# Another order for the middle of a planned RWKV-7 and mixer kernel, and transposes as pairs of 64-row blocks

## The chip, the core and the metric

The kernel runs on one core of a Trainium2 chip. The metric is device time in microseconds of one launch, read and written in HBM. Times are the median of several executions; a profile is one further execution, recorded by the hardware profiler.

The core has five engines with a queue each. PE (TensorE) does matrix products and transposes and writes to PSUM, a memory of eight banks. DVE (VectorE) and ACT (ScalarE) read PSUM and write to SBUF. POOL (GpSimd) works on SBUF alone. SP (SyncE) issues most DMAs. Each engine takes its queue in order and waits for others by semaphores.

## What is computed

Two stages. The first is a recurrence over 768 steps for 4 batches of 8 heads with a state of 40 by 40 per head:

```python
for t in range(S):
    y[:, :, t] = np.einsum('bhd,bhde->bhe', rt, state)
    Sa = np.einsum('bhde,bhe->bhd', state, at)
    state_decay = state * wt[:, :, None, :] - np.einsum('bhd,bhe->bhde', Sa, bt)
    state = state_decay + np.einsum('bhd,bhe->bhde', vt, kt)
```

The second takes the heads side by side (x, 768 by 320 for each batch) through a mixer:

```python
theta = x @ w_theta
zr, zi = x * np.cos(theta), x * np.sin(theta)
y = np.einsum('ts,bsd->btd', w_tok_r, zr) + np.einsum('ts,bsd->btd', w_tok_i, zi)
u = x + y
return u + np.maximum(u @ w_ch, 0.0)
```

## The kernel before

**Tiling.** The 768 steps of a batch are six chunks of 128, so there are 24 chunks, numbered 0 to 23 through all batches. Inside a chunk the recurrence is written as products of triangular score matrices; from chunk to chunk a state (`gt`, and its turned copy `gd`) is handed on. For chunk i the operations are, with the names that the text uses (kind and chunk, `tkb8`):

- loads `lw lk lb la lv` and `loadr` (SP);
- `ln`, `cs`, `exp`, `cx` or `wi`, `ew`: sums of the logarithms of w and their exponentials;
- `kb` (two), `ah`, `v`, `r`: products or casts into padded bf16 tiles with 64 columns for each head, mostly on POOL;
- transposes on PE: `tkb` (eight blocks of 128x128 from k and b), `ta` and `tv` (four each), `tr` (eight, for two chunks at once), `nut` (four), and for the mixer `xt` and `ut` (five each for two chunks); `wt` (six) turns rows of the token weights. Each is copied from PSUM to SBUF by ACT or DVE: `ekb ea ev er enut ext eut ewt`;
- scores on PE: `spsi sphi slv slu`, eight matmuls of 64 rows and 128 columns each. The two halves of the rows hold two heads, and write two different PSUM banks. `mpsi mphi mlv mlu` multiply them by a triangular mask on DVE, or copy them on ACT, after which `sel` cuts the triangle on POOL;
- the recurrence: `x0`, `nx`, `nu`, `enu`, `gt`, `egt`, `wgt`, `gd`, `egd`; the readout `y` and `ex`;
- the mixer: `th` and `eth` (theta), `sin` (sine and cosine on ACT, with a change of activation table), `z` (x times cosine or sine, on POOL or DVE, two for each chunk), `row` (the products over tokens, six steps for each chunk), `uadd`, `ch`, `oo`, `st`.

`thj` and `chj` are the last part of a product that is shared by two chunks, on 64 rows.

**The order.** The code adds 1602 operations to a plan with what each reads and writes (`Plan.add`, L161), then emits them in the order of a list of numbers, `ORDER` (L26). Only the order within an engine's queue has an effect; waits between engines follow from the data. `HOMES` (L122) gives each new PSUM tile its bank, in order of emission. `PICK` (L138) names the operations that run on their second choice of engine. `WARM` (L145) puts some matmuls on a constant ahead of early operations. All of these lists are written out in the file.

**PSUM.** Banks 0 to 3 are two tiles of two banks each (`doubles`), which the scores use; banks 4 to 7 are four single tiles. A transpose takes one bank. `scores` (L558) writes `ps(p)[:, q]`, bank q for half q of the rows. A transpose in the code before goes through `transpose_pairs` or a loop of its own:

```python
nc.tensor.transpose(out=dst[:, c:c + 128], in_=pair(src, g), identity=ident)
```

ACT copies its result as 32-bit words, DVE as 16-bit elements (`copy_words` and `copy_halves`, both used by `evac`).

Of the kernel before, what the change touches and what calls it, by code (L numbers as in the profile page):

```python
# [26 lines left out]
    0, 7, 3, 6, 1, 2, 20, 8, 21, 23, 24, 4, 27, 9, 32, 30, 5, 22, 31, 33, 12, 25, 26, 34, 11,  # L27
    28, 10, 69, 35, 36, 29, 70, 37, 18, 47, 44, 40, 19, 48, 72, 45, 38, 41, 71, 49, 73, 39, 46,
    98, 119, 76, 99, 58, 14, 42, 100, 74, 57, 15, 13, 120, 122, 101, 50, 121, 79, 75, 51, 123,
    53, 106, 102, 107, 131, 108, 80, 52, 16, 77, 109, 132, 125, 78, 43, 103, 81, 17, 110, 134,  # L30
    126, 111, 133, 82, 56, 84, 137, 54, 104, 124, 138, 112, 129, 83, 85, 87, 130, 88, 127, 55,
    156, 86, 128, 59, 157, 89, 146, 184, 143, 90, 147, 105, 158, 61, 97, 60, 139, 187, 159,
    135, 62, 144, 148, 164, 96, 188, 160, 165, 191, 140, 93, 136, 145, 161, 166, 141, 91, 185,
    167, 213, 186, 92, 194, 214, 149, 189, 142, 162, 168, 150, 215, 163, 169, 190, 216, 195,
    152, 221, 170, 234, 151, 246, 192, 222, 235, 193, 237, 217, 95, 236, 202, 238, 218, 94,
    196, 203, 197, 63, 241, 155, 247, 171, 267, 248, 219, 239, 199, 198, 172, 220, 223, 205,
    249, 200, 240, 271, 64, 244, 272, 242, 299, 245, 201, 154, 273, 224, 243, 300, 173, 301,
    261, 206, 254, 274, 302, 225, 174, 262, 303, 279, 153, 175, 258, 306, 176, 255, 212, 259,
    263, 280, 250, 177, 204, 281, 256, 211, 275, 496, 282, 260, 320, 226, 251, 305, 257, 208,
    252, 276, 264, 283, 253, 317, 207, 227, 349, 327, 265, 277, 497, 328, 304, 309, 278, 329,  # L40
    498, 284, 266, 310, 270, 499, 330, 350, 285, 307, 351, 268, 318, 286, 354, 308, 269, 331,
    352, 500, 311, 361, 332, 319, 287, 314, 353, 312, 209, 336, 333, 539, 362, 210, 337, 289,
    356, 288, 315, 363, 313, 322, 290, 364, 338, 355, 291, 387, 325, 292, 339, 316, 365, 540,
    388, 359, 366, 389, 541, 357, 360, 340, 390, 341, 382, 358, 391, 321, 116, 503, 113, 501,
    542, 412, 373, 181, 342, 334, 376, 374, 502, 392, 367, 411, 326, 504, 377, 375, 506, 335,
    393, 368, 505, 323, 178, 369, 545, 524, 394, 378, 370, 507, 517, 525, 413, 508, 372, 526,
    384, 371, 509, 395, 416, 396, 527, 532, 417, 528, 397, 510, 511, 514, 529, 544, 117, 595,
    512, 572, 533, 415, 383, 530, 118, 398, 573, 515, 596, 513, 554, 385, 399, 534, 531, 574,
    418, 597, 401, 535, 400, 516, 575, 414, 402, 543, 379, 324, 404, 114, 567, 598, 536, 403,
    546, 548, 115, 380, 581, 642, 576, 582, 555, 601, 549, 577, 381, 583, 599, 66, 386, 550,  # L50
    584, 537, 557, 568, 600, 551, 182, 522, 558, 602, 183, 585, 586, 538, 619, 578, 561, 587,
    419, 179, 518, 559, 547, 604, 519, 556, 427, 180, 428, 421, 429, 605, 560, 420, 606, 520,
    423, 552, 607, 626, 553, 562, 434, 422, 627, 564, 435, 425, 436, 565, 563, 643, 628, 424,
    437, 644, 610, 566, 629, 426, 613, 645, 603, 588, 611, 630, 231, 523, 571, 521, 589, 438,
    430, 570, 698, 635, 631, 646, 612, 439, 431, 636, 632, 440, 608, 745, 432, 614, 699, 647,
    609, 746, 700, 675, 648, 747, 637, 433, 615, 676, 616, 701, 293, 569, 633, 677, 748, 634,
    651, 649, 638, 678, 590, 652, 684, 296, 579, 685, 679, 617, 639, 228, 620, 621, 580, 653,
    706, 657, 591, 654, 680, 592, 618, 686, 650, 593, 661, 703, 687, 594, 441, 622, 711, 702,
    640, 442, 681, 712, 662, 688, 655, 658, 705, 656, 689, 659, 641, 663, 660, 682, 704, 664,
    690, 749, 667, 683, 665, 691, 68, 709, 692, 707, 67, 710, 729, 668, 65, 670, 672, 666, 708,  # L60
    694, 693, 750, 624, 695, 730, 719, 713, 697, 751, 720, 731, 696, 232, 732, 294, 233, 297,
    714, 721, 295, 733, 738, 298, 229, 734, 739, 715, 716, 230, 740, 735, 717, 754, 450, 752,
    451, 778, 755, 718, 346, 625, 452, 779, 453, 741, 343, 623, 756, 881, 780, 454, 757, 408,
    882, 781, 742, 405, 673, 671, 764, 883, 767, 765, 669, 782, 884, 444, 722, 455, 783, 443,
    768, 456, 766, 445, 784, 446, 736, 457, 885, 785, 458, 760, 737, 743, 447, 459, 753, 448,
    786, 787, 887, 744, 761, 796, 788, 769, 758, 460, 759, 789, 763, 461, 888, 762, 790, 462,
    797, 912, 463, 792, 791, 913, 793, 723, 770, 795, 892, 771, 914, 794, 674, 893, 915, 886,
    772, 802, 890, 464, 891, 803, 773, 347, 465, 916, 348, 344, 799, 917, 905, 805, 409, 345,
# [133 lines left out]
def mm(n):  # L202
    return max(n / 2.4 + 2.5, 25.0)
# [853 lines left out]
```

## Time and profile before

| | us |
|---|---|
| runs | 197.72, 198.29, 202.19 |
| median | 198.29 |
| span of the profiled execution | 197.8 |

The profile comes from an execution of its own, whose whole time is not listed; its span, from the first to the last instruction, lies between the lowest and the middle one of the three runs. On the profile's page, engines are named as above, with PEld for the weight loads that run beside the matmuls. An engine's busy time is the union of its instructions; for PE the end of each matmul is modelled. A line such as L391 may be that of a helper and stand for several kinds of operations. In the groups, a row gives line, engine, operation, what is written from what, shapes, count, total time, the mean of one in ns, and the idle time ahead of them with what ended it. In a timeline, a row gives start, length of the group, engine, line and count.

### The profile page before, as it was taken

The page shows a single profiled execution, that of the slowest core. Times are in us where ns is not written, and L with a number is a line of the kernel's source. Part 1 is how long each engine was busy: PE and PEld are TensorE (multiplying, and loading weights), DVE is VectorE, ACT ScalarE, POOL GpSimd, SP SyncE. Part 2 cuts the span into 40 slices and gives each one's busy share as a digit, 9 for nine tenths or more (in the row PEclk, how much of TensorE's full clock was granted, in tenths as well). Part 3 has the DMA queues.
Part 4 walks back from the last instruction along what each step waited for, and adds up shares of the span by engine and source line. Part 5 has one row for each costly group of instructions (what it writes and reads, how often), then busy time and mean ns, then how long its engine had stood idle before and what let it go on. Part 6 is the DMA issues. An engine that isn't in the chain of part 4 may idle for free.

```text
span 197.8 us, 8019 instructions
## 1 busy us (share of the span) xinstructions
PE 187.6 (95%) x3288; PEld 150.3 (76%) x3288; DVE 164.3 (83%) x261; ACT 151.7 (77%) x337; POOL 145.1 (73%) x210
## 2 busy tenths in 40 slices
PE   7888999999989999999999999999999999999992
PEld 6776787777768788878878888888887878767661
DVE  5269899999989999888887988999999988675453
ACT  3584979799889988979988598888998986575111
POOL 8267544679879999699799939769699697558100
PEclk9999999999999999999999999999999999999999
DMA  6999879989999999999998899988998274863055
GB/s 119 210 212 163 154 161 196 182 166 197 233 174 173 207 171 185 190 185 223 153 210 168 153 187 170 188 148 169 182 155 163 43 177 102 87 194 104 0 191 174
DMA packets 134644, 32.75 MB, mean 166 GB/s; under 512 B 124816, under 2 KB 134608, under 8 KB 134608
## 3 DMA queue, kind: packets, MB, share of 16 engines
q1 hardware_dynamic: 131680, 29.19, 75.1%
q0 software_dynamic: 2784, 2.97, 9.6%
q8 instruction: 25, 0.41, 0.9%
q10 hardware_dynamic: 144, 0.08, 0.1%
q14 instruction: 11, 0.09, 0.1%
HBM read 29.54 MB, written 3.93 MB: 169 GB/s over the span
## 4 chain that ended last, share of the span: by engine, by line
PE 68%; DMA 9%; ACT 8%; SPq 6%; DVE 3%; issue 3%; POOL 1%; ACTq 0%; DVEq 0%; POOLq 0%
PE ps_s L881 17%; PE ps_s L391 10%; PE ps_d L569 9%; PE ps_s L763 5%; SPq L409 4%; DMA raw_w<-in_w_dram 3%; DMA raw_kb<-in_k_dram 3%; PE ps_s L711 3%; PE ps_s L652 2%; PE ps_s L629 2%; SPq L421 2%; DMA raw_r<-in_r_dram 2%; PE ps_s L538 2%; PE ps_s L773 2%; ACT cs L850 2%
## 5 line engine op out<-in xcount | busy, mean ns | idle before, releaser
L429 POOL TENSOR_TENSOR kb<-raw_kb,ex 128x320 bf16<-128x320 f32 x46 | 36.8, 811 | 9.7 <-DMA raw_kb<-in_k_dram 3.3
L881 PE MATMUL ps_s<-zr,wtok_r 128*128 128x320 bf16 x132 | 37.6, 299 | 0.0
L881 PE MATMUL ps_s<-zi,wtok_i 128*128 128x320 bf16 x132 | 37.5, 299 | 0.0
L578 DVE TENSOR_TENSOR lamu<-ps_d,mask_p 128x1024 bf16<-128x1024 f32 x22 | 26.8, 1219 | 1.7 <-PE ps_d L569 1.6
L578 DVE TENSOR_TENSOR psi<-ps_d,mask_p 128x1024 bf16<-128x1024 f32 x22 | 26.8, 1218 | 1.6 <-PE ps_d L569 1.4
L578 DVE TENSOR_TENSOR lamv<-ps_d,mask_p 128x1024 bf16<-128x1024 f32 x17 | 20.7, 1218 | 2.6 <-PE ps_d L569 1.8
L429 POOL TENSOR_TENSOR ah<-raw_a,we 128x320 bf16<-128x320 f32 x22 | 19.0, 866 | 3.6 <-DMA raw_a<-in_a_dram 1.6
L578 DVE TENSOR_TENSOR phi<-ps_d,mask_n 128x1024 bf16<-128x1024 f32 x17 | 20.7, 1218 | 0.9 <-PE ps_d L569 0.8
L865 POOL TENSOR_TENSOR zi<-cs,xp 128x320 bf16<-128x320 f32 x21 | 16.9, 816 | 3.3 <-ACT cs L850 3.3
L881 PEld LDWEIGHTS <-wtok_r 128*128 128x128 bf16 x144 | 14.0, 97 | 4.5
L569 PE MATMUL ps_d<-aT,kbT 64*128 64x128 bf16 x384 | 17.1, 217 | 0.2
L881 PEld LDWEIGHTS <-wtok_i 128*128 128x128 bf16 x144 | 14.1, 98 | 3.5
L391 PE MATMUL ps_s<-wide,kb 128*128 128x128 bf16 x184 | 15.0, 223 | 1.0 <-POOL kb L429 0.7
L865 POOL TENSOR_TENSOR zr<-cs,xp 128x320 bf16<-128x320 f32 x19 | 15.3, 810 | 0.7 <-ACT cs L850 0.7
L667 POOL TENSOR_TENSOR gt<-sum,ex 128x320 bf16<-128x320 f32 x13 | 9.5, 733 | 8.0 <-DVE sum L663 4.8
L800 PE MATMUL ps_s<-kb,lamv 128*128 128x40 bf16 x192 | 15.0, 180 | 0.0
L802 PE MATMUL ps_s<-kb,lamu 128*128 128x40 bf16 x192 | 14.9, 179 | 0.0
L569 PEld LDWEIGHTS <-kbT 64*128 64x128 bf16 x384 | 11.8, 94 | 3.1 <-ACT kbT L394 1.0
L800 PEld LDWEIGHTS <-lamv 128*128 128x128 bf16 x192 | 13.2, 96 | 0.6
L887 DVE TENSOR_TENSOR up<-ps_s,xp 128x320 bf16<-128x320 f32 x22 | 10.7, 488 | 3.5 <-PE ps_s L881 3.1
L435 POOL CAST r<-raw_r 128x640 bf16<-128x640 f32 x12 | 8.6, 720 | 6.5 <-DMA raw_r<-in_r_dram 6.5
L445 ACT ACTIVATE lw<-raw_w 128x320 bf16<-128x320 f32 x24 | 11.4, 475 | 2.6 <-DMA raw_w<-in_w_dram 2.6
(176 smaller groups left out, 606.7 us busy)
## 6 DMA issues: line engine op xcount, KB each, us to landing
raw_w<-in_w_dram SPq DMA_DIRECT2D x24, 160.0 KB, 4.1
raw_v<-in_v_dram SPq DMA_DIRECT2D x24, 160.0 KB, 3.9
raw_a<-in_a_dram SPq DMA_DIRECT2D x24, 160.0 KB, 4.2
raw_kb<-in_k_dram SPq DMA_DIRECT2D x24, 160.0 KB, 3.7
raw_kb<-in_b_dram SPq DMA_DIRECT2D x24, 160.0 KB, 4.0
raw_r<-in_r_dram SPq DMA_DIRECT2D x24, 160.0 KB, 4.4
out_dram<-oo SPq DMA_DIRECT2D x9, 160.0 KB, 2.0
wrow_i<-in_moe_w_tok_i_dram POOLq DMA_DIRECT2D x6, 192.0 KB, 5.3
```

The costliest lines, as they stand in the source:

```text
L391: nc.tensor.transpose(out=dst[:, c:c + 128], in_=pair(src, g), identity=ident)
L429: pool = ("POOL", lambda: nc.gpsimd.tensor_tensor(out=dst, in0=in0, in1=in1, op=ALU.mult))
L445: add("ACT", "ln", i, lambda: nc.scalar.activation(out=paired(lw)[:, :, :, 0:D], in_=paired(raw_w[s4]), func=AF.Ln), 473, [("raw_w", s4)], ...
L569: nc.tensor.matmul(t[:, q, g, :], lhsT=lhs[g][rows(q)], rhs=rhs[g][rows(q)], start=True, stop=True)
L578: add("DVE", kindm, i, lambda: nc.vector.tensor_tensor(out=flat, in0=whole(), in1=mask.to_broadcast([128, 2 * G, 128]), op=ALU.mult), 1217 ...
L667: add("POOL", "wgt", i, lambda: nc.gpsimd.tensor_tensor(out=new_state, in0=sum_t, in1=wm.to_broadcast([128, 8, D]), op=ALU.mult), 830, [(" ...
L763: nc.tensor.matmul(ps(pk)[:, 0:DM], lhsT=lhs[:, 3 * c + kt, :], rhs=wt[:, 3 * c + kt, :], start=kt == 0, stop=kt == 2, skip_group_check=n ...
L800: nc.tensor.matmul(o, lhsT=lamv[:, p, g, :], rhs=kb[:, 0, h, 0:D], start=first, stop=False, skip_group_check=True)
L802: nc.tensor.matmul(o, lhsT=lamu[:, p, g, :], rhs=kb[:, 1, h, 0:D], start=False, stop=True, skip_group_check=True)
L865: pool = ("POOL", lambda: nc.gpsimd.tensor_tensor(out=dst, in0=in0, in1=in1, op=ALU.mult))
L881: nc.tensor.matmul(acc(), lhsT=wtok[nm][j][:, s], rhs=zs[c][:, s], start=n == 0 and c == 0, stop=n == NT - 1 and c == 1)
L887: add("DVE", "uadd", q, lambda: nc.vector.tensor_tensor(out=u, in0=acc(), in1=x, op=ALU.add), 488, [pk, x_key(q)], [u_key(q)], at="row")
```

## The change

Three things change together.

1. **Lists.** `ORDER`, `HOMES`, `PICK` and `WARM` are replaced. Read queue by queue, PE's list of 596 operations is the same for the first 144 and the last 149; DVE's for the first 61, ACT's for the first 106, POOL's for the first 47 and SP's for the first 61. `PICK` moves some 40 evacuations, casts, products and masks to another engine: of the `z` products, the two of chunk 17 (on 1194 and 1198) and two of chunk 21 (1462, 1463) go from DVE to POOL. `WARM` keeps its counts and names a bank.
2. **PSUM.** One tile of eight banks takes the place of two doubles and four singles; `HOMES` may give any bank, or any two neighbours.
3. **Split transposes.** A transposing operation has a second choice. If `PICK` names it, it takes two banks, and each 128x128 block is transposed in two parts: rows 0 to 63 into the first bank and rows 64 to 127 into the second, each with 64 columns. The copy out of PSUM then reads both banks in pieces of 64 elements (or 32 words). 39 operations use it: 8 `tkb`, 7 `ta`, 6 `tr`, 5 `tv`, 5 `xt`, 5 `wt`, 2 `nut` and 1 `ut`, of chunks 8 to 20.

```diff
-PICK = [
-    25, 31, 37, 39, 40, 48, 49, 75, 80, 85, 86, 115, 118, 130, 172, 180, 193, 203, 204, 222,
...
-WARM = {21: 25, 30: 4, 33: 1, 28: 8, 41: 11}
+WARM = {21: (0, 25), 30: (1, 4), 33: (2, 1), 28: (1, 8), 41: (1, 11)}
...
-        for n in PICK:
-            self.ops[n].eng, self.ops[n].fn = self.ops[n].alts[0]
+        for n, m in PICK.items():
+            o = self.ops[n]
+            o.eng, o.fn = o.alts[m - 1][:2]
+            if o.eng == "PE":
+                o.new = (o.new[0], 2)
...
-    doubles = [psum.tile([128, 2, 512], FP32, name=f"ps_d{i}") for i in range(DOUBLE // 2)]
-    singles = [psum.tile([128, 512], FP32, name=f"ps_s{i}") for i in range(BANKS - DOUBLE)]
+    banks = psum.tile([128, BANKS, 512], FP32, name="banks")
...
-        return doubles[h[0] // 2] if len(h) == 2 else singles[h[0] - DOUBLE]
+        return banks[:, h[0]:h[0] + 2] if len(h) == 2 else banks[:, h[0]]
...
+    def turned(kind, i, key, srcs, reads, cost, at="tile"):
+
+        def go():
+            if not split(key):
+                t = ps(key).bitcast(BF16)
+                for m, src in enumerate(srcs()):
+                    nc.tensor.transpose(out=t[:, m * 128:m * 128 + 128], in_=src, identity=ident)
+                return
+            for m, src in enumerate(srcs()):
+                for c in range(2):
+                    nc.tensor.transpose(out=ps(key)[:, c].bitcast(BF16)[:, m * 64:m * 64 + 64],
+                                        in_=src[rows(c)], identity=ident[rows(c), rows(c)])
+        add("PE", kind, i, go, cost, reads, [key], at=at, new=(key, 1), tail=tail(128),
+            alts=(("PE", go),))
...
+        def copy(op, out, dt, w):
+            one, src = n * w // 64, ps(psk) if w == 32 else ps(psk).bitcast(BF16)
+            if not split(psk):
+                at = (part or 0) * one
+                op(out=out, in_=src[:, at:at + one])
+            elif part is not None:
+                op(out=out, in_=src[:, part, 0:one])
+            else:
+                op(out=out.rearrange("p (n c w) -> p c n w", c=2, w=w),
+                   in_=src[:, :, 0:one // 2].rearrange("p c (n w) -> p c n w", w=w))
+        act = ("ACT", lambda: copy(nc.scalar.copy, dst.bitcast(FP32), FP32, 32))
+        dve = ("DVE", lambda: copy(nc.vector.tensor_copy, dst, BF16, 64))
...
+                for c in range(2):
+                    nc.tensor.transpose(out=tokens(ps(pr)[:, c].bitcast(BF16)[:, 0:512], q),
+                                        in_=src[rows(c)], identity=ident[rows(c), rows(c)])
```

The last lines are those of `turn_runs`, which does `tr`; the other transposes go through `turned`. Before the change 67 blocks of 64-row operations stand in PE's list (each a run of scores, `thj` or `chj` between 128-row ones), after it 78.

More of the change, by code (lines that the diff above doesn't have):

```diff
@@ L508, in tr @@
             n = 4 * len(srcs)
[L509 to L510 removed]
+            turned(kind, i, p, lambda: pairs_of(srcs), skeys, n * mm(128))
             evac(eng, kinde, i, p, dst, n * 128, writes=[dkey])
@@ L706, in feature_major @@
         n = len(blocks)
-        def go():
-            t = ps(p).bitcast(BF16)
-            for m, src in enumerate(blocks):
-                nc.tensor.transpose(out=t[:, m * 128:m * 128 + 128], in_=src, identity=ident)
-        add("PE", kind, q, go, n * mm(128), skeys, [p], at=at, new=(p, 1), tail=tail(128))
+        turned(kind, q, p, lambda: blocks, skeys, n * mm(128), at)
         evac("ACT", kinde, q, p, dst[:, 0:n, :].rearrange("p a b -> p (a b)"), n * 128,
@@ L1015 @@
         if o.idx in WARM:
-            t = ps(o.new[0])
-            t = t[:, 0] if len(t.shape) == 3 else t
-            for _ in range(WARM[o.idx]):
-                nc.tensor.matmul(t[:, 0:128], lhsT=busy[:, 0:128], rhs=busy[:, 0:128],
+            at, n = WARM[o.idx]
+            for _ in range(n):
+                nc.tensor.matmul(banks[:, at, 0:128], lhsT=busy[:, 0:128], rhs=busy[:, 0:128],
                                  start=True, stop=True, skip_group_check=True)
```

77 lines of the change are left out of this document (30 added, 47 removed), and 237 rows, old and new, of tables (HOMES, ORDER, PICK).

## Prediction

> **What bounds the kernel now.** I read the page first, then busy time in three stretches: up to the first matrix operation whose place changes, from there to the last one, and the rest. The columns of the stretches are length, then PE, PEld, DVE, ACT and POOL, then granted clock, DMA share and GB/s.
>
> ```profile
> span 197.8 us, 8019 instructions
> ...
> PE 187.6 (95%) x3288; PEld 150.3 (76%) x3288; DVE 164.3 (83%) x261; ACT 151.7 (77%) x337; POOL 145.1 (73%) x210
> ...
> PE 68%; DMA 9%; ACT 8%; SPq 6%; DVE 3%; issue 3%; POOL 1%; ACTq 0%; DVEq 0%; POOLq 0%
> ```
>
> ```profile
> 0.00:60.40 60.40, 54.53 (x1001) 44.43 (x1002) 49.62 (x85) 46.69 (x113) 41.12 (x73) 1.00 0.94 181
> 60.40:152.80 92.40, 91.86 (x1732) 75.50 (x1733) 84.17 (x123) 81.31 (x182) 81.19 (x112) 1.00 0.99 178
> 152.80:198.00 45.20, 41.23 (x560) 30.40 (x558) 30.48 (x54) 23.68 (x45) 22.77 (x27) 1.00 0.48 119
> ```
>
> PE leads in the chain and in the stretch concerned; the clock is full, so no term comes from it. But "busy" counts each matmul to its modelled end, some 0.2 us, while the next starts much sooner. So I went on to the timeline, for the distance from start to start (columns: start, length of the group, engine, line, shapes, count).
>
> ```profile
> 104.38 0.20 PE L652 MATMUL ps_s<-v,kb 128*128 128x80 bf16 x1
> 104.42 0.20 PE L652 MATMUL ps_s<-nu,kb 128*128 128x80 bf16 x1
> 104.55 0.40 PE L569 MATMUL ps_d<-rT,vT 64*128 64x128 bf16 x8
> 104.80 0.39 PE L569 MATMUL ps_d<-rT,nuT 64*128 64x128 bf16 x8
> 105.12 0.19 PE L800 MATMUL ps_s<-kb,lamv 128*128 128x40 bf16 x1
> 105.16 0.18 PE L802 MATMUL ps_s<-kb,lamu 128*128 128x40 bf16 x1
> 105.18 0.18 PE L800 MATMUL ps_s<-kb,lamv 128*128 128x40 bf16 x1
> 105.21 0.18 PE L802 MATMUL ps_s<-kb,lamu 128*128 128x40 bf16 x1
> ...
> 105.67 0.24 PE L464 MATMUL ps_s<-ones,lw 128*128 128x2 bf16 x4
> ...
> 117.36 0.31 PE L773 MATMUL ps_s<-wth,xT 64*128 64x320 bf16 x2
> 117.50 0.61 PE L569 MATMUL ps_d<-aT,kbT 64*128 64x128 bf16 x16
> ...
> 154.86 0.61 PE L391 MATMUL ps_s<-wide,kb 128*128 128x128 bf16 x8
> ...
> 161.95 0.30 PE L881 MATMUL ps_s<-zr,wtok_r 128*128 128x320 bf16 x1
> 162.09 0.30 PE L881 MATMUL ps_s<-zi,wtok_i 128*128 128x320 bf16 x1
> 162.22 0.30 PE L881 MATMUL ps_s<-zr,wtok_r 128*128 128x320 bf16 x1
> ```
>
> Four things are to be seen.
> - The step of a 128-row matmul follows its columns: 0.135 us for 320 (161.95, 162.09, 162.22), 0.035 for 80, 0.025 for 40. Eight of 128 columns take 0.61 with the last one's 0.22 in it: 0.056 each.
> - Two matmuls on 64 rows each share a step: the L773 pair of 320 columns lasts 0.31, as one alone does, and sixteen of 128 columns take the same 0.61 as eight 128-row ones.
> - Going over to 64 rows costs: 104.42 to 104.55 is 0.13 where the step is 0.035, so about 0.095.
> - Going back costs as much: four pairs from 104.80 at 0.056 end at 105.02, the next starts at 105.12. A block of 64-row work costs about 0.19 us for its two ends.
>
> With these steps I add up the 1732 matmuls of the second stretch, counts from the groups by form: 202 of 320 or 328 columns 27.5, 416 of 128 columns 23.3, 216 of 80 7.6, 460 of 40 or 2 11.5, 208 pairs of 128 columns 11.6, 11 pairs of 320 1.5, and 31 blocks 5.9. That is 88.9 of 92.4 us. So PE's own sequence sets the pace in this stretch, with some 3.5 us of waits, most of them too short to show as idle time.
>
> **The change, part by part. The transposes.** Of the changed choices 39 are transposing operations that now use the split form: 228 transposes (`tkb` 64, `tr` 48, `wt` 30, `ta` 28, `xt` 25, `tv` 20, `nut` 8, `ut` 5), all in the second stretch. Each 128-column matmul of 0.056 us becomes two 64-row, 64-column ones, one per half of the array's rows. No row shows 64 columns; between 80 (0.035) and 40 (0.025) lies 0.029. If the halves share a step, as the L773 pair does, a transpose saves 0.027, and 228 save 6.2 us. The bound on the other side: if 0.025 is the least time per instruction, whichever rows it uses, two halves cost 0.050 and 228 save 1.4. I take 6.2, because the pair of 320 columns is the nearest row in kind.
>
> The Trainium skill, "TensorE: Matmul & The Clock Gate", Back-to-back issue gap, gives every matmul up to 64 columns one floor of about 25 ns; its "TensorEngine Tiling (Array Packing)", Instruction Overhead, says not to tile along a dimension that is already small. By that rule the sum would be the second one. The rows agree on the floor for 128 rows (40 columns step by 0.025, and four of 2 columns take 0.24, no less); none shows it for two halves.
>
> **The 64-row blocks.** Read in order, PE's list has 67 blocks of 64-row work before and 78 after: some split transposes join a neighbouring score block, others stand alone (`tkb` of chunks 16, 17 and 18). 11 more at 0.19 cost 2.1 us. PE's net is 6.2 - 2.1 = 4.1 us less, 84.8 for the stretch.
>
> **The evacuations** of the split transposes read two PSUM banks in pieces. Rows of such copies:
>
> ```profile
> L546 ACT COPY rT<-ps_s 128x256 f32<-128x256 f32 x24 | 8.2, 378 | 1.6 <-DVE sx L482 0.8 <-PE ps_s L538 0.7
> L394 ACT COPY vT<-ps_s 128x256 f32<-128x256 f32 x21 | 7.6, 371 | 2.3 <-PE ps_s L391 1.2 <-PE ps_s L538 0.8
> L397 DVE COPY kbT<-ps_s 128x1024 bf16<-128x1024 bf16 x8 | 5.5, 686 | 0.3 <-PE ps_s L391 0.2
> L397 DVE COPY aT<-ps_s 128x512 bf16<-128x512 bf16 x8 | 3.4, 420 | 0.8 <-PE ps_s L391 0.7
> L578 DVE TENSOR_TENSOR psi<-ps_d,mask_p 128x1024 bf16<-128x1024 f32 x22 | 26.8, 1218 | 1.6 <-PE ps_d L569 1.4
> L623 DVE CAST nx<-ps_s 128x320 bf16<-128x320 f32 x2 | 1.0, 486 | 0.2 <-PE ps_s L616 0.2
> ```
>
> On ACT a copy in two pieces (rT) takes 7 ns more than a whole one (vT): nothing. On DVE 4 `ekb`, 3 `ea` and 1 `enut` read split banks. They could lose the pace of two 16-bit elements per cycle that 686 for 1024 shows against psi's 1218: up to 0.53 for each `ekb` and half of that for the four others, 3.2 us in all. A gain has no source, since the same elements move. I take 0: the inner runs stay whole.
>
> **Engines changed.** In the stretch DVE takes over 16 instructions (one mask of 1.22, one `kbT` copy 0.69, three 512-element copies at 0.42, one `wtok` copy 0.55, ten 320-column copies at 0.48 to 0.49: 8.6 us) and gives up 13 (6.7 us), so it carries 1.9 us more: 84.2 becomes 86.1. PE's 84.8 and the 3.5 of waits are still 88.3, so DVE just fits, at 97%. That is the cover for the transposes' gain, and the case where it fails is priced below. ACT gets casts from POOL in exchange.
>
> **The order.** It decides how much of the 3.5 us of waits stays, and a split tile takes two of the eight PSUM banks, 39 more takeovers. Bounds: all waits gone (-3.5) and waits doubled (+3.5). I take 0. Loads change places in SP's queue too, but of all waits in the stretch one row names a DMA, and POOL can bear it: 0. In the first stretch every queue keeps its order and only bank numbers change: 0.
>
> ```profile
> POOL r L435 <- DMA raw_r<-in_r_dram: 0.5, 1, 0.5
> ```
>
> **The tail.** PE's list is the same there, but the two `z17` and two `z21` products that DVE made go to POOL:
>
> ```profile
> 154.70 0.18 PE L802 MATMUL ps_s<-kb,lamu 128*128 128x40 bf16 x1
> ...
> 154.99 1.58 POOL L429 TENSOR_TENSOR kb<-raw_kb,ex 128x320 bf16<-128x320 f32 x2 [1.56 <-ACT aT L394]
> ...
> 158.48 1.56 POOL L865 TENSOR_TENSOR zi<-cs,xp 128x320 bf16<-128x320 f32 x2
> 159.99 1.05 POOL L865 TENSOR_TENSOR zr<-cs,xp 128x320 bf16<-128x320 f32 x1
> 161.00 1.04 POOL L865 TENSOR_TENSOR zi<-cs,xp 128x320 bf16<-128x320 f32 x1
> ...
> 159.77 1.62 DVE L864 TENSOR_TENSOR zr<-cs,xp 128x320 bf16<-128x320 f32 x2
> ...
> 181.12 0.79 POOL L865 TENSOR_TENSOR zr<-cs,xp 128x320 bf16<-128x320 f32 x1 [0.35 <-ACT cs L850]
> 181.86 0.79 POOL L865 TENSOR_TENSOR zr<-cs,xs 128x320 bf16<-128x320 f32 x1
> 183.37 0.79 POOL L865 TENSOR_TENSOR zi<-cs,xs 128x320 bf16<-128x320 f32 x1 [0.72 <-ACT cs L845]
> ```
>
> Today the last `z17` ends at 162.04, and the row product that reads it starts at 162.22. Six in a row from 158.48, at 0.75 each (1.56 for two, overlapping), end at 163.05. PE waits 1.0 us; 1.6 if two more run at 1.05. The queue can't start earlier, because `kb23` overwrites what `y19` reads until its last matmul (154.70), and PE's list is the same from before that. Nothing behind on PE is ready out of turn, so this 1.0 is paid. For `z21` POOL is idle 0.35 and 0.72 between its products, which takes most of the extra; between 0 and 1.0, I take 0.
>
> **Sum.** -6.2 + 2.1 + 1.0 = -3.1 on a span of 197.8: 194.7. The shown runs are 197.72, 198.29 and 202.19, so the span lies 0.5 under the median. On the median: **195.2 us**. Its own range is 193.4 to 197.4, with half of the order's bounds and 0.4 more from the tail.
>
> **The rivals.** For the first, rows of the chain of waits (start, length, piece):
>
> ```profile
> 91.09 1.10 ACT cs L850
> ...
> 96.30 1.99 ACT cs L850 x2
> ...
> 98.68 1.28 ACT L1024
> ```
>
> 1. *The order also closes waits.* ACT sets the chain's pace in a part of the stretch, with the sines and their tables, and the change takes `mphi12`, `nx11`, `nx12`, `enu11`, `eth10` and three copies of chunk 13 off it. For it speaks that PE has only 84.8 us of its own; against, that DVE is then at 86.1. With 2.7 of the 3.5 gone: 192.5.
> 2. *The halves pay 0.025 each* (the floor named above): -1.4 + 2.1 + 1.0 = +1.7, 200.0. The shared step at 320 columns speaks against it, the equal step at 40 and 2 columns for it.
> 3. *DVE becomes the bound* (the other side). If its queue can't be packed closer than now, 84.17 of 92.40 or 91%, the stretch lasts 86.1 / 0.91 = 94.6, 2.2 us longer. With 1.0 from the tail: 201.5; with the slower split copies 3.5 more, 205.0. It decides from the point at which DVE's work between two matmuls that feed and need it exceeds PE's, first from `mlu7` to `ex9`, ahead of `xt8`. Against it: PE keeps 2.2 us of slack over DVE.
> 4. *One tile for all banks makes unrelated banks wait for each other*, so the split does nothing that can be seen: if a tenth of the 335 bank takeovers in the stretch waited for a strange copy of 0.37 (the vT row), that is +12: 210. Nothing in the profile shows such a tile (`ps_d` already holds two banks without such waits).
>
> **How the numbers follow.** Chances: the forecast 0.46, rival 1 0.20, rival 2 0.14, rival 3 0.16, rival 4 0.04. Two per cent, about what a measurement of this kernel tells from no change, means below 194.3 or above 202.3. Faster: 0.18 of rival 1 and 0.13 of the forecast's range, 0.31. Slower: rival 4, 0.08 of rival 3 and 0.02 of rival 2, 0.14. The rest, 0.55, is within. Faster and slower than before both have weight, so the likeliest case's own range stands above. The range for 8 in 10 runs from 192.3 to 201.5; left out are rival 4, the upper half of rival 3 and the lowest part of rival 1.
>
> **What would show it.** In the timeline after: split transposes as pairs, eight of them (16 matmuls) in about 0.39 us with the last one's length in it (0.57 would be rival 2); 0.095 at each edge of a block; the second stretch at about 88 us, with DVE at 86; PE waiting about 1 us on `zi` at the row products after `y20`. Wrong would be: PE waits on DVE in groups of the second stretch (rival 3), new waits at PSUM takeovers everywhere (rival 4), or a copy of a split `kbT` on DVE far from 686 ns.

## The result and the profile after

| | us | ratio to the kernel before, 95% interval |
|---|---|---|
| before, 10 runs | 198.68 (median) | |
| after, 10 runs | 196.94 (median, 195.57 to 198.22) | 0.9928, 0.9899 to 0.9956 |
| after, 9 more runs | 197.63 | 0.9924, 0.9887 to 0.9961 |
| after, 12 more runs | 198.05 | 0.9947, 0.9904 to 0.9990 |
| profiled execution of after | 197.58, its span 195.9 | |

The kernel got about 0.7% faster, 1.3 us (0.9933 is the mean of the three ratios, and the reference for the experiments). The ratios are taken from undisturbed executions alone, so they are not the quotients of the medians. The forecast was 195.2 with a range of its own from 193.4 to 197.4: 196.94 lies inside it, but the forecast fall is 3.1 us and the measured one 1.3. It was right in sign and about twice too large in size.

The page of the profile after: span, busy time, and the shares of the chain of waits.

```profile
span 195.9 us, 8473 instructions
...
PE 184.3 (94%) x3516; PEld 145.4 (74%) x3516; DVE 163.3 (83%) x260; ACT 150.6 (77%) x336; POOL 145.1 (74%) x211
...
PE 61%; DMA 12%; POOL 9%; ACT 6%; DVE 4%; SPq 4%; issue 2%; ACTq 0%; DVEq 0%; POOLq 0%
```

PE's share of the chain fell from 68% to 61%; DMA and POOL took it over (9% to 12%, 1% to 9%). PE is still the busiest engine, but more often it stands and waits.

Busy time in the same three stretches as before: up to the start of `ta8`, from there to the start of `tv21`, and the rest (columns as in the prediction).

```profile
0.00:59.97 59.97, 54.15 (x1000) 44.39 (x1001) 50.62 (x86) 46.40 (x112) 40.85 (x73) 1.00 0.95 183
59.97:149.82 89.85, 88.43 (x1959) 70.49 (x1959) 84.18 (x126) 80.44 (x181) 77.62 (x107) 1.00 0.96 174
149.82:196.00 46.18, 41.77 (x562) 30.57 (x558) 28.55 (x50) 23.73 (x45) 26.67 (x34) 0.98 0.58 133
```

The middle is 89.85 us long instead of 92.40, where 88 was forecast; DVE is busy for 84.18 of it, no more than before. Split transposes in PE's timeline:

```profile
106.76 0.44 PE L404 MATMUL banks<-wide,up 128*128 128x128 bf16 x5
107.13 0.29 PE L408 MATMUL banks<-wide,ah 64*128 64x64 bf16 x8
107.65 0.41 PE L408 MATMUL banks<-wide,kb 64*128 64x64 bf16 x16 [0.23 <-ACT uT L422]
107.99 0.19 PE L829 MATMUL banks<-kb,lamv 128*128 128x40 bf16 x1
```

Eight split transposes (x16) take 0.41 with the last one's 0.19 in it, where 0.39 was forecast and 0.57 by rival 2. The five of 128 columns from 106.76 end their steps at 107.04 (5 x 0.056), and the 64-row block starts 0.09 later. Its sixteen end theirs near 107.90 (eight steps of 0.029, the first of them 0.039), and the next 128-row matmul starts 0.09 later. Both prices stand as forecast.

For the whole middle I went through all starts on PE. Each matmul has its step from its shape, as the starts in these traces show it (136 ns for 320 columns, 69 for 160, 56 for 128, 35 for 80, 29 for a pair of 64 on two halves, 25 for 40 and for 2; other widths by the straight line through these), and 92 to 95 ns more at an edge between 128 and 64 rows; the sum is PE's own sequence, and what the distances exceed it by are waits. All such figures below are made like that.

| us | first stretch | middle | own steps in it | waits in it | tail |
|---|---|---|---|---|---|
| before | 60.33 | 92.44 | 88.9 | 3.6 | 41.25 |
| after | 59.97 | 89.86 | 85.1 | 4.7 | 42.23 |
| after, 2nd profile | 58.84 | 90.74 | 85.2 | 5.6 | 42.53 |
| after, 3rd profile | 58.91 | 91.23 | 85.2 | 6.1 | 43.02 |

PE's own sequence fell by 3.7 us, and the waits of the middle rose by 1.9 us (the mean of three profiles, against a single one of before); the tail is longer by 1 us or more. The first stretch swings by 1.5 us in kernels that have it alike, so it is no effect of the change.

The border between first stretch and middle hides a part of this. In the first profile PE waits 0.91 us on `ah8` just ahead of `ta8`:

```profile
59.97 0.29 PE L408 MATMUL banks<-wide,ah 64*128 64x64 bf16 x8 [0.91 <-POOL ah L456]
```

In the other two it does not; there the middle starts 1.1 us earlier, and a wait of about 1.5 us stands inside it, at 82 us (shown below). From the start to `tv21` the three executions nearly agree, 149.83, 149.58 and 150.14 us, where 152.77 stood before: up to there 2.9 of the 3.7 us came through.

The tail, in PE's timeline and then in POOL's:

```profile
152.12 0.32 PE L713 MATMUL banks<-wide,gt 128*128 128x80 bf16 x4 [0.18 <-POOL gt L701]
...
158.38 0.30 PE L910 MATMUL banks<-zi,wtok_i 128*128 128x320 bf16 x1
158.80 0.30 PE L910 MATMUL banks<-zr,wtok_r 128*128 128x320 bf16 x1
...
159.90 0.30 PE L910 MATMUL banks<-zr,wtok_r 128*128 128x320 bf16 x1
160.30 0.30 PE L910 MATMUL banks<-zi,wtok_i 128*128 128x320 bf16 x1
```

```profile
157.21 2.28 POOL L894 TENSOR_TENSOR zr<-cs,xp 128x320 bf16<-128x320 f32 x3
159.46 0.79 POOL L894 TENSOR_TENSOR zi<-cs,xp 128x320 bf16<-128x320 f32 x1
```

Row products step by 0.137, but twice by 0.42 and 0.40: PE waits 0.28 and 0.27 on `z` products that POOL now makes four in a row; the last ends at 160.25, and its reader starts at 160.30. With 0.34 by the starts ahead of `gd20`, whose `gt` stands behind another `z` on POOL, that makes about 0.9, near the forecast's 1.0. But that other `z` is on POOL before the change too, and the 0.34 stays when the four products go back to DVE (experiment 6), so only the 0.28 and 0.27 are theirs.

The largest waits of the middle do not stand at the same places in the three profiles. In the first one PE waits on `ah13` and, as in the other two, on `kbT13`:

```profile
95.50 0.29 PE L408 MATMUL banks<-wide,ah 64*128 64x64 bf16 x8 [0.25 <-POOL ah L456]
97.76 0.62 PE L603 MATMUL banks<-aT,kbT 64*128 64x128 bf16 x16 [0.33 <-DVE kbT L426]
```

The second of them is the split `kbT` copy that moved to DVE; it takes 0.69, as the whole ones did, and PE has nothing else in its list meanwhile:

```profile
97.01 0.69 DVE L426 COPY kbT<-banks 128x1024 bf16<-128x1024 bf16 x1 [0.23 <-PE banks L408]
```

Behind `ah13` stands a load. Here is SP's issue of `la13` and POOL's queue, after; then the same issue before:

```profile
86.11 0.59 SPq L436 DMA_DIRECT2D raw_a<-in_a_dram  x1
```

```profile
85.67 1.14 POOL L989 DMA_DIRECT2D wrow_i<-in_moe_w_tok_i_dram  x2
86.79 1.08 POOL L989 DMA_DIRECT2D wrow_r<-in_moe_w_tok_r_dram  x2
...
94.58 0.86 POOL L456 TENSOR_TENSOR ah<-raw_a,we 128x320 bf16<-128x320 f32 x1 [3.42 <-DMA raw_a<-in_a_dram]
```

```profile
82.79 0.58 SPq L409 DMA_DIRECT2D raw_a<-in_a_dram  x1
```

The new order issues this load 3.3 us later, and it is over 8 us under way, beside four loads of token weights that POOL issues in the same two microseconds. These neighbours alone do not decide it: in the second profile the same load, issued at 86.26 beside the same four, lands after 4.1 us. There it is `lw13` that takes 9.1 us, for which ACT stands still, and PE behind it:

```profile
81.36 0.47 ACT L472 ACTIVATE lw<-raw_w 128x320 bf16<-128x320 f32 x1 [1.45 <-DMA raw_w<-in_w_dram]
```

```profile
82.21 0.40 PE L404 MATMUL banks<-wide,nu 128*128 128x128 bf16 x4 [1.55 <-ACT nu L667]
```

### The profile page after: what moved, and what is told of

Read it like the earlier page. It is cut to its first block, busy times and chain, and to the rows that moved or that the text cites. A ratio compares the mean times of both kernels' runs of the same rounds, so it can differ in the third digit from the quotient of the medians.

```text
span 195.9 us, 8473 instructions
## 1 busy us (share of the span) xinstructions
PE 184.3 (94%) x3516; PEld 145.4 (74%) x3516; DVE 163.3 (83%) x260; ACT 150.6 (77%) x336; POOL 145.1 (74%) x211
## 4 chain that ended last, share of the span: by engine, by line
PE 61%; DMA 12%; POOL 9%; ACT 6%; DVE 4%; SPq 4%; issue 2%; ACTq 0%; DVEq 0%; POOLq 0%
PE banks L910 16%; PE banks L603 9%; PE banks L404 8%; PE banks L792 5%; DMA raw_a<-in_a_dram 4%; DMA raw_kb<-in_k_dram 4%; SPq L436 3%; PE banks L408 3%; DMA uT<-up 2%; PE banks L569 2%; PE banks L663 2%; POOL kb L456 2%; PE banks L686 2%; PE banks L802 2%; DMA raw_v<-in_v_dram 2%
## 5 line engine op out<-in xcount | busy, mean ns | idle before, releaser
L910 PE MATMUL banks<-zr,wtok_r 128*128 128x320 bf16 x144 | 41.0, 300 | 0.2
L910 PE MATMUL banks<-zi,wtok_i 128*128 128x320 bf16 x144 | 40.8, 299 | 0.1
L612 DVE TENSOR_TENSOR lamu<-banks,mask_p 128x1024 bf16<-128x1024 f32 x22 | 26.8, 1219 | 1.5 <-PE banks L603 0.8
L612 DVE TENSOR_TENSOR psi<-banks,mask_p 128x1024 bf16<-128x1024 f32 x22 | 26.8, 1219 | 0.8 <-PE banks L603 0.7
L612 DVE TENSOR_TENSOR phi<-banks,mask_n 128x1024 bf16<-128x1024 f32 x18 | 21.9, 1216 | 1.6 <-POOL r L462 1.3
L612 DVE TENSOR_TENSOR lamv<-banks,mask_p 128x1024 bf16<-128x1024 f32 x17 | 20.7, 1219 | 1.6 <-PE banks L603 1.0
L603 PE MATMUL banks<-aT,kbT 64*128 64x128 bf16 x384 | 17.2, 217 | 0.9 <-DVE kbT L426 0.3
L829 PE MATMUL banks<-kb,lamv 128*128 128x40 bf16 x192 | 14.9, 180 | 0.0
L831 PE MATMUL banks<-kb,lamu 128*128 128x40 bf16 x192 | 14.8, 179 | 0.0
L831 PEld LDWEIGHTS <-lamu 128*128 128x128 bf16 x192 | 13.0, 96 | 0.0
```

Of the source, the lines that this page charges most:

```text
L603: nc.tensor.matmul(t[:, q, g, :], lhsT=lhs[g][rows(q)], rhs=rhs[g][rows(q)], start=True, stop=True)
L612: add("DVE", kindm, i, lambda: nc.vector.tensor_tensor(out=flat, in0=whole(), in1=mask.to_broadcast([128, 2 * G, 128]), op=ALU.mult), 1217 ...
L829: nc.tensor.matmul(o, lhsT=lamv[:, p, g, :], rhs=kb[:, 0, h, 0:D], start=first, stop=False, skip_group_check=True)
L831: nc.tensor.matmul(o, lhsT=lamu[:, p, g, :], rhs=kb[:, 1, h, 0:D], start=False, stop=True, skip_group_check=True)
L910: nc.tensor.matmul(acc(), lhsT=wtok[nm][j][:, s], rhs=zs[c][:, s], start=n == 0 and c == 0, stop=n == NT - 1 and c == 1)
```

## The experiments

My theory after the result: the split pays what was forecast on PE, and PE then runs into its feeders (loads, POOL, PSUM banks), which hand part of it back. The rivals: the order makes the gain and the split is hidden; DVE has become the bound; the halves do not need to be neighbours.

**1. The split alone, in the new order.** The 39 numbers of split transposes are taken out of `PICK`; order, engines and first banks stay.

```diff
-    ... 172: 1, 182: 1, 183: 1, 193: 1, ...
+    ... 172: 1, 193: 1, ...
```

> Changed kernel with all 39 split transposes undone (whole 128x128 blocks, one bank each), order and engines kept. Theory (PE's own sequence sets the pace of the middle, and the split shortens it): 228 transposes at 0.027 us come back, +6.2, and 78 blocks of 64-row work become 75, -0.6: about 5.6 us longer than the changed kernel if no wait shrinks, 4 to 5.6 with the waits of the middle taken into account, so 201 to 202.5 us, slower than the kernel before by 2 to 4 us. Rival (the new order and the engines bring the gain, the split is hidden): within 1 us of the changed kernel, 196 to 198 us.

Measured: 200.71 us, 1.0084 (1.0054 to 1.0115), that is 3.0 us more than after (1.0084 - 0.9933, of 199). The middle:

```profile
59.05:152.28 93.23, 92.84 (x1735) 75.46 (x1731) 85.90 (x127) 81.17 (x182) 77.65 (x106) 1.00 0.97 177
```

Own steps are 90.4 and waits 2.8. So the split saves 5.3 us of PE's steps (5.6 forecast) and brings 3.0 us of time, 57%. Without it the new order is slower than the old one by 0.8%: its 75 blocks where there were 67 are 8 x 0.19 = 1.5 us more of PE's own steps. The rival falls, and so does the size of the theory: I had expected 4 to 5.6. By the intervals the 3.0 is good to about 0.7 us.

**2. The split alone, in the old order.** `ORDER` and engines of before, the 39 split; the banks are given out by a search for the fewest late takeovers.

```diff
+PICK = {n: 1 for n in (before's list + the 39 of after)}
+ORDER = (before's list)
```

> The kernel before in order and engines, with the same 39 transposes split; the banks are given out anew. PE's list then has 84 blocks of 64-row work where it had 67. Theory: -6.2 + 17 x 0.19 = -3.0 us of PE's own sequence, and no z17 term, so about 195.7 us (194.5 to 197), as good as the changed kernel or better. Rival (the split needs the new order, which joins its blocks and feeds PE earlier): the gain is lost in waits, 198 to 199.5 us.

> The kernel before in order and engines with all 39 transposes split, once more. The runs will say 1.006 to 1.014 again. By the theory (the order is fitted to the lengths: POOL and DVE take their queues in the old order, and what PE needs next stands behind what it freed early), PE's steps are 86.5 us and its waits in the middle 7 to 9 us, at a few places of 0.4 to 1 us each, above all where PE waits on gt of POOL or on a product that stands behind another in its queue. Rival (the eight banks are too few for 39 more takeovers): the waits are spread over many transposes, each below 0.2 us.

Measured: 1.0102 (1.0063 to 1.0142) and 1.0103 (1.0041 to 1.0166), 2 us slower than before, although PE's own steps fell by 2.5 us. In the second profile the middle is 94.33, with 86.4 of own steps and 8.0 of waits. PE's timeline, rows with a releaser:

```profile
68.60 0.20 PE L686 MATMUL banks<-v,kb 128*128 128x80 bf16 x1 [0.81 <-DVE psi L612]
...
75.65 0.40 PE L603 MATMUL banks<-aT,kbT 64*128 64x128 bf16 x8 [0.31 <-DVE sum L697]
...
121.14 0.41 PE L408 MATMUL banks<-wide,kb 64*128 64x64 bf16 x16 [0.24 <-ACT lamv L614]
...
134.29 0.41 PE L572 MATMUL banks<-wide,r 64*128 64x64 bf16 x16 [0.55 <-DVE phi L612]
...
149.57 0.20 PE L644 MATMUL banks<-gt,aT 128*128 128x80 bf16 x1 [0.60 <-POOL gt L701]
```

`gt8` does not read `psi`, nor the transpose of `r` `phi`: what they wait for is the bank that this mask still reads. The first four are bank takeovers, only the last is data. These five make 2.5 of the 8.0 us; by the starts on PE, 17 waits of 0.13 to 0.87 us make 5.5, and the others were not sorted by their cause. So it is neither the few places of the theory nor the many below 0.2 us of the rival, and the largest waits have mostly the rival's cause: 39 more banks taken, in an order that has no slack for them. That holds for this bank plan; a better one was not tried.

**3. Only those splits that join a block in the old order** (16 operations, 83 transposes, 67 blocks as before).

```diff
+PICK = {n: 1 for n in (before's list + 16 of the 39)}
+ORDER = (before's list)
```

> The kernel before in order and engines, with only those 16 of the 39 transposing operations split (83 transposes) that stand next to other 64-row work in its list, so that the 67 blocks stay 67; the banks are given out anew. PE's own steps fall by 83 x 0.027 = 2.2 us. Theory (without blocks to pay for, and with fewer pieces that come at another time, the split gains in the old order too): 0.5 to 1.5 us less than the kernel before, 0.992 to 0.997. Rival (the old order is fitted to the old lengths, and any shift of them costs more in waits than the split saves, as with all 39): 1.00 to 1.01.

Measured: 0.9976 (0.9939 to 1.0013). Own steps fell by 1.9 us to 87.0, waits rose by 2.6 to 6.2 in the one profile, with the same two places (0.83 on `psi`'s bank, 0.82 on `gt`). Between theory and rival: no loss, and no gain that can be told from none.

**4. Halves apart.** Each split operation first does all its blocks on rows 0 to 63, then all on the other half.

```diff
-            for m, src in enumerate(srcs()):
-                for c in range(2):
+            for c in range(2):
+                for m, src in enumerate(srcs()):
```

> Changed kernel with the same split transposes, but each operation issues all its blocks on rows 0 to 63 first and then all on rows 64 to 127, so that no two neighbours on PE use different rows. Theory (two halves share a step only where they stand next to each other): a step of 0.025 to 0.029 for every half, 228 x 0.025 to 0.029 = 5.7 to 6.6 us more on PE, 202 to 203.5 us; eight split transposes then take about 0.6 us instead of 0.4. Rival (64 columns on 64 rows are simply cheap, about 0.014 each, wherever they stand): no change, 197 us.

Measured: 198.71 us, 0.9979 (0.9947 to 1.0010), 0.9 us more than after (0.9979 - 0.9933), with 2.2 us more of own steps; both theory and rival were wrong. The timeline of PE:

```profile
78.93 0.41 PE L604 MATMUL banks<-rT,vT 64*128 64x128 bf16 x8
79.26 0.53 PE L408 MATMUL banks<-wide,kb 64*128 64x64 bf16 x16
79.72 0.31 PE L793 MATMUL banks<-wth,xT 128*128 128x320 bf16 x1
...
95.99 0.19 PE L408 MATMUL banks<-wide,up 64*128 64x64 bf16 x1
96.01 0.19 PE L408 MATMUL banks<-wide,wrow_i 64*128 64x64 bf16 x1
96.02 0.19 PE L408 MATMUL banks<-wide,up 64*128 64x64 bf16 x1
96.04 0.19 PE L408 MATMUL banks<-wide,wrow_i 64*128 64x64 bf16 x1
...
96.18 0.19 PE L408 MATMUL banks<-wide,ah 64*128 64x64 bf16 x1
96.18 0.19 PE L408 MATMUL banks<-wide,up 64*128 64x64 bf16 x1
```

Sixteen take 0.53 instead of 0.41, not 0.62 (16 steps of 0.029 less one, and 0.19). Their starts show why: four at 0.029, then eight that share steps two by two, then four at 0.029. The second half starts while the first still has three blocks to start. And at 95.99 `up`, which stands behind `wrow_i` in PE's list, starts between its last blocks: lower half of the one beside the upper half of the other. So by these starts PE lets a matmul on the other half of the rows overtake, by three. An operation of four blocks loses about 0.01 us by the order of its halves (one of them, at 124.74, does not overtake and loses 0.1), one of eight 0.12 us. The Trainium skill, "TensorE: Matmul & The Clock Gate", Part 3: Packing small matmuls, has matmuls start and end strictly in the order of the program, and tiles on other rows about 4 ns apart; the 4 ns agree (3 to 4 ns within a pair after the change), the strict order does not hold in these rows.

That 2.2 us more of PE's steps cost 0.9 us of time (good to about 0.8) points the same way as experiment 1: about half of a change in PE's steps comes through. All 39 splits keep their banks here, and the waits are 3.7 us, so the takeovers of split tiles alone do not make the 4.7 to 6.1 of after.

**5. More work on one engine at a time.** Small instructions that nobody needs, spread evenly over the middle.

```diff
         if o.fn is not None:
             o.fn()
+        if o.idx in EXTRA:
+            nc.vector.memset(spare, 1.0)
```

(on ACT `nc.scalar.copy(out=spare, in_=busy)`, on POOL `nc.gpsimd.memset`.) The changed kernel ran beside them:

> The changed kernel once more, beside the three that follow: 0.990 to 0.996 of the kernel before, as measured. Its profile shows which waits of the middle come back in a second execution: where PE's own steps of the middle are 85.2 us again, waits of 5 to 6 us (5.8 in the first profile) speak for feeders that PE has caught up with; under 4 us would mean that the first profile was a poor one.

> Changed kernel with 12 more instructions on DVE, spread evenly over the middle (a fill of a 128x128 bf16 tile that nobody reads, 0.165 us each by the row of the same shape, 2.0 us in all). If DVE's queue is what the middle now waits for: 1.5 to 2 us more than the changed kernel (a ratio of about 1.001 to 1.003 where that has 0.993). If PE's own sequence still sets the pace and DVE has room: at most 0.5 us more. Theory: between the two, 1 to 2 us, because DVE is busy for 85.2 of 91 us.

> Changed kernel with 8 more copies on ACT, spread evenly over the middle (128x128 bf16 into a tile that nobody reads, 0.2 to 0.3 us each, about 2 us in all). Theory (ACT has room, busy for 80.9 of 91 us): at most 0.7 us more than the changed kernel. Rival (ACT's latency is in the chain that feeds PE, so each copy delays it): 1.5 to 2 us more.

> Changed kernel with 10 more fills on POOL, spread evenly over the middle (128x128 bf16, 0.205 us each by the row of the same shape, 2.0 us in all). Theory (POOL has room, busy for 78.8 of 91 us, and its products for a chunk are made ahead): at most 0.7 us more than the changed kernel. Rival (POOL, behind the loads of a and k, is what PE has caught up with): 1.5 to 2 us more.

| | ratio, interval | against 0.9933 | middle in the profile |
|---|---|---|---|
| DVE, 2.0 us more | 0.9968, 0.9932 to 1.0004 | +0.7 us | 89.92 |
| ACT, 2.5 us more | 0.9927, 0.9897 to 0.9956 | -0.1 us | 89.90 |
| POOL, 2.0 us more | 0.9954, 0.9921 to 0.9986 | +0.4 us | 90.84, in an execution 1.8 us over its median |

No engine answers with the 1.5 to 2 us of a bound, and the three middles are no longer than those of after (89.86 to 91.23). DVE is nearest to one, but below the 1 to 2 us that I had expected; its 0.7 is good to about 0.8 us, so that a part of the waits is DVE's is not excluded. Rival 3 of the forecast, a middle of 94.6 us, falls by the measured 89.9 to 91.2 already.

**6. The z products back on DVE.**

```diff
+    1194: 1, 1198: 1, 1462: 1, 1463: 1
```

> Changed kernel with the two z17 and the two z21 products back on DVE, all else kept. Theory (the tail's term): PE's row products after y20 then wait about 1 us less on POOL, so the time falls by 0.8 to 1.1 us against the changed kernel (a ratio to the kernel before of about 0.988 where the changed kernel has 0.993). Rival: DVE, which has to take two more products in the middle, or something else behind them, gives the microsecond back, and the ratio stays at 0.992 to 0.994.

Measured: 197.34 us, 0.9898 (0.9863 to 0.9933): 0.7 us under after, a little less than the theory's 0.8 to 1.1, and the intervals meet. The two waits at the row products are gone in its profile; the 0.34 ahead of `gd20` stays. The tail of this one execution, 1.75 us over the median of its runs, is not shorter all the same: 43.43, because PE waits for `nuT21`, which comes by a DMA transpose that SP issues:

```profile
164.97 0.41 PE L603 MATMUL banks<-rT,nuT 64*128 64x128 bf16 x8 [1.55 <-DMA nuT<-nu]
```

**7. Loads and their order.** `lw13` and `la13` earlier in SP's queue:

```diff
-lb11 lv10 lk12 la11 lk11 lb12 lw13 la12 lb13 loadr12 lv12 lk13 lv13 loadr12 la13
+lb11 lw13 lv10 lk12 la11 lk11 lb12 la12 la13 lb13 loadr12 lv12 lk13 lv13 loadr12
```

> Changed kernel with two loads of chunk 13 further ahead in SP's queue: w behind the first load for chunk 11 (four places earlier) and a right behind that for chunk 12 (six places earlier). In the profiles so far one or the other of them lands just before its use (0.1 us), after 6 to 9 us under way, and PE's larger waits of the middle (0.4 to 1.7 us at a time, near 80 or 94 us) stand behind them. Theory (part of what PE saves is given back to these loads): 0.5 to 1.5 us less than the changed kernel, a ratio of 0.985 to 0.990, and no wait over 0.4 us on PE from 78 to 98 us. Rival (another feeder stands just behind, or other loads are pushed back as far): 0.992 as before.

> The changed kernel with the two loads of chunk 13 earlier, once more. Theory: 0.985 to 0.990 of the kernel before (the changed kernel: 0.9926), and a middle of about 89.5 us in the profile. Rival: 0.992, and the 89.3 us of the first profile was chance.

Measured: 0.9900 (0.9836 to 0.9964) and 0.9952 (0.9912 to 0.9992). The two profiles agree with the theory:

```profile
60.13:149.33 89.20, 88.22 (x1964) 70.43 (x1960) 84.58 (x126) 80.83 (x182) 77.73 (x107) 1.00 0.99 180
```

```profile
58.89:148.14 89.25, 88.21 (x1965) 70.42 (x1960) 84.70 (x127) 80.87 (x182) 77.41 (x106) 1.00 0.98 177
```

Waits are 4.0 and 4.1, the large ones at 80 and 94 us gone. The runs do not: their mean is 0.9926, 0.1 us under after's. So the loads explain waits in single executions, and that they cost the median anything is not shown.

Four token-weight loads earlier in POOL's queue, away from the loads of chunk 13:

```diff
-wgt8 kb10 kb10 v11 ah10 wdma5 wdma4 kb11 wdma5 wdma4
+wgt8 wdma5 wdma4 wdma5 wdma4 kb10 kb10 v11 ah10 kb11
```

> Changed kernel with the four loads of token-weight rows, which POOL issues at 72 to 75 us among the loads of chunks 12 and 13, moved ahead to about 66 us in POOL's queue, where a load takes 4 us instead of 7 to 9. Theory (the loads of chunk 13 are late because they share the DMA engines with these): as above, 0.3 to 1.2 us less than the changed kernel, w of chunk 13 taking 5 to 6 us instead of 6 to 9. Rival (POOL's queue pays for four issues of 0.57 us ahead of the products of chunk 10, or DMA has no free time at 66 us either): 0 to 1 us more.

Measured: 1.0024 (0.9987 to 1.0061), 1.8 us more than after: worse than the rival's 0 to 1.

With it, the two loads of chunk 13 and the z products together:

```diff
+    (the edits of 6 and both edits of 7 in one kernel)
```

> Changed kernel with the two loads of chunk 13 earlier, the four token-weight loads earlier and the z17 and z21 products back on DVE. Theory, the three being independent: the sum of the three effects, 1 to 3 us less than the changed kernel, 0.977 to 0.987 of the kernel before. Rival: the middle is held at about 91 us by several feeders together, and only the tail's 0.5 to 1 us remain, 0.988 to 0.990.

Measured: 1.0030 (0.9994 to 1.0066): the loss of the weights stays. Its profile shows where POOL's queue pays, and PE with it:

```profile
68.72 0.61 POOL L989 DMA_DIRECT2D wrow_i<-in_moe_w_tok_i_dram  x1
69.32 1.07 POOL L989 DMA_DIRECT2D wrow_r<-in_moe_w_tok_r_dram  x2
70.36 0.56 POOL L989 DMA_DIRECT2D wrow_i<-in_moe_w_tok_i_dram  x1
70.90 1.61 POOL L456 TENSOR_TENSOR kb<-raw_kb,ex 128x320 bf16<-128x320 f32 x2
```

```profile
72.57 0.92 PE L404 MATMUL banks<-wide,kb 128*128 128x128 bf16 x7 [1.58 <-POOL kb L456]
```

Four issues hold POOL for 2.2 us ahead of `kb10`, and PE waits 1.58 for it.

The loads of chunk 13 earlier and no split (both edits as above):

> The changed kernel with the two loads of chunk 13 earlier and all 39 transposes whole. Theory (the loads stand in the way only of a PE that has become faster): the same as the order without split and without moved loads, 1.006 to 1.010, so that the split is worth 3.5 to 4.5 us once the loads are out of its way, where it was worth 3.1 with them in it. Rival (the loads are late for the new order whatever PE does): 1.000 to 1.004, and the split is worth 2.5 to 3 us still.

Measured: 1.0101 (1.0039 to 1.0163), waits of 2.8 us as without moved loads: no gain without the split, as the theory had it. A difference to e5 of 3.5 us (1.0101 - 0.9926) lies at the lower end of the expected 3.5 to 4.5, but its interval holds the 3.0 of experiment 1 too.

**8. What the terms suggest, together:** z products on DVE, `lw13` and `la13` earlier, and `lw9` ahead of `lb8`.

```diff
-loadr6 loadr6 lb8 loadr8 lw9 lk8
+loadr6 loadr6 lw9 lb8 loadr8 lk8
```

> The changed kernel with the two loads of chunk 13 earlier, w of chunk 9 in front of the loads of chunk 8 in SP's queue (in about half of the profiles it lands just before its use, and PE then waits 1.0 to 1.5 us near 54 us), and the z17 and z21 products back on DVE. Theory: 0.5 to 0.8 (loads of 13) + 0.3 to 0.7 (w of 9) + 0.5 to 1.0 (z) less than the changed kernel: 0.980 to 0.987 of the kernel before. Rival (another load stands right behind, and the waits move on): 0.987 to 0.990, the z products alone.

> The changed kernel beside the next one: 0.990 to 0.996 of the kernel before, a middle of 90.8 to 91.2 us in the profile with 5.5 to 6 us of waits.

> The version with three loads moved ahead and the z17 and z21 products on DVE, once more. Theory: 0.982 to 0.989, 0.6 to 1.8 us under the changed kernel of the same chip, with a middle of 89.3 to 90 us and no wait at row12 and row14. Rival (the two shorter middles were chance): 0.987 to 0.991, by the z products alone, and a middle of 91 us.

Measured: 0.9868 (0.9806 to 0.9931) and, beside the changed kernel's 0.9947, 0.9902 (0.9858 to 0.9945). It beats the kernel before by 1%, 2 us. Against after it gains some 0.9 us in its pair of runs, about what the z products brought alone (0.9898); that the three loads bring anything is not shown. `lw9` was not moved alone; the first stretch is 59.51 and 59.75 us, in the range of the others. Its tails are 41.52 and 41.64, the middles 88.99 and 89.88; in the second one the wait has moved on to the next load (POOL, then PE):

```profile
78.27 0.80 POOL L456 TENSOR_TENSOR kb<-raw_kb,ex 128x320 bf16<-128x320 f32 x1 [1.35 <-DMA raw_kb<-in_k_dram]
```

```profile
79.13 0.41 PE L408 MATMUL banks<-wide,kb 64*128 64x64 bf16 x16 [0.83 <-POOL kb L456]
```

## Why the prediction was half right

- **The transposes, -6.2, and the blocks, +2.1: right.** PE's own steps of the middle fell by 3.7 us where the two make 4.1. Where the other 0.4 stayed I did not look for. Pairs step by 0.029, but the first of a run often by 0.039, which counts here as a wait. That the pair shares its step was a choice by the nearest row, and the rows bear it out. Rival 2 fell by 0.41 us for eight transposes.
- **The evacuations, 0: right.** 0.69 for a split `kbT` on DVE, 0.686 for a whole one.
- **The engines, DVE at 86.1: too high.** Its busy time in the middle is 84.2 to 84.9 in the three profiles. The lengths of its rows add up to 91.1 us before and 92.7 in the second profile of after, 1.6 us more, near the forecast's 1.9; but neighbouring rows overlap, so busy time rose by only 0.6. Twelve more instructions of 2.0 us cost 0.7 us, within the scatter. Rival 3 fell by the length of the middle.
- **The order, 0: wrong, and the step that failed.** The sum carried PE's saving on its own steps over to the time whole, with "I take 0" for the waits between -3.5 and +3.5; they rose by 1.9 us (3.6 to 4.7, 5.6 and 6.1). Where the wait on `ah8` falls into the first stretch, as in the first profile, they rose by 1.1. The forecast treated waits as a property of the order. Experiments 1 and 4 show that they go with PE's pace: in the new order 2.8 us of waits with 90.4 of steps, 3.7 with 87.4 (halves apart), 5.5 on average with 85.2. Waits for feeders grew when PE got faster, and about half of what it saved came through. Which feeder is met changes from one execution to the next: a load of chunk 13, `kb14`, `ah8`. The loads are part of the mechanism, but their share of the median stays open.
- **SP's loads, 0: wrong in kind.** One row named a DMA before; after, `lw13` or `la13` lands just before its use in all three profiles, as the new order issues `la13` 3.3 us later, and ACT is ready for `lw13` at about 81 us where it took it at 85.6 before.
- **The tail, +1.0: right in size, in part by luck.** 42.23 where 41.25 stood in the first profile. The moved products account for 0.28 and 0.27 of it; 0.34 ahead of `gd20` is there without them, and the tails of 41.52 and 41.64 with the products back still hold it. The 42.53 and 43.02 of the other profiles hold 0.35 and 0.79 us more of waits on `uT`, which comes by DMA transposes, a wait that the forecast did not have; with the 1.7 us on `nuT` in experiment 6 they make the tail swing by more than the term.
- **From span to time: mis-sized, but no part of the change.** I put 0.5 between them, by the median. Every profiled execution lists its time about 1.7 us over its span (197.58 and 195.9 here), so the one before probably took 199.5, 0.8 over the median of ten runs. This moves both ends alike; the sum took 3.1 off the median as off the span. Span against span the change is -1.9, -1.9 and -0.8 us, in the mean -1.5. By terms that is -3.7 for the steps (forecast -4.1), +1.9 for the waits (0), +1.3 for the tail (+1.0) and -1.1 for the first stretch (0), which is taken as chance: the early starts into the middle are those with the longer waits in it.
- **Rival 4: its 12 us did not come,** and no wait between tiles that share no bank was found among the waits that were read. One split in the new order waits 0.27 us for its own two banks in all three profiles (`wt11` on the mask `lamv`, at about 95 us). In the old order bank takeovers are the largest waits, at tiles that do share the bank.

## What to carry to other kernels

When the busiest engine has others at 86 to 94% beside it, do not carry a saving on its own steps over to the time whole. Here 5.3 us of PE's steps became 3.0 us of time, and 2.2 us of extra steps cost 0.9; half is a first guess from this one kernel, not a rule. Before an order is blamed or praised, run the four combinations of old and new order with and without the new instructions: the split alone was 1% slower, the order alone 0.8% slower, and both together 0.7% faster. And compare executions from the start to a common point as well as by stretches: a wait that one execution pays ahead of a border another pays behind it.

## What the runs showed of the hardware

- Two 64-row matmuls of 64 columns on different halves start 3 to 4 ns apart in most pairs, and a pair takes 0.029 us, so the step of 0.025 us that 128-row matmuls of 40 and of 2 columns keep is not a least time for every instruction.
- In experiment 4 PE starts matmuls out of the order of its list when they are on the other half of the rows: three ahead, and across operations (95.99 to 96.04).
- A load of 160 KB (`la13`) was 8.3 us under way in the first profile (issued at 86.11, four token-weight loads of 192 KB beside it), 8.6 in the third and 4.1 in the second, with the same four beside it each time; the page's medians for such loads in the first run are 3.7 to 4.3 us. What makes the difference was not found.
